# Sums in place between a quad's first products, and six second products in one run, in the experts of a fused attention, mixture and feed-forward kernel

## The chip, the cores and the metric

The kernel runs on one core of one Trainium2 chip. The metric is the device time of one execution, in microseconds. The profile comes from one execution recorded by the hardware profiler; its engines are PE (the matrix engine; PEld is its loading of weights), DVE (the vector engine), ACT (the scalar engine), POOL (GpSimd) and SP (the queue that issues most loads).

## What is computed

Three layers follow each other. An attention with random features turns `q`, `k`, `v` (4 batches, 8 heads, 576 rows, 64 columns) into 2304 rows of 512. Then a mixture of eight experts, in which every expert sees every row and a table `P` of weights (made by eight rounds of row and column scaling) mixes them, and last a feed-forward layer with `h - tanh(h)`:

```python
logits = x @ w_gate
P = np.exp(logits - logits.max())
for _ in range(8):
    P /= P.sum(1, keepdims=True) + 1e-09
    P /= P.sum(0, keepdims=True) + 1e-09
    P *= N / E
for e in range(E):                      # E = 8, w1[e] is 512 x 1024, w2[e] 1024 x 512
    h = np.maximum(x @ w1[e], 0.0)
    out += P[:, e:e + 1] * (h @ w2[e])
...
h = x @ w_in                            # 512 x 2048
return (h - np.tanh(h)) @ w_out         # 2048 x 512
```

## The kernel before, in words

**Numbers.** Every fp32 matrix is split into a high and a low half, and each product is three matmul passes (high by high, high by low, low by high).

**The experts (about 167 to 1677 us).** The 2304 rows are cut into three blocks of 768 (`NSB`), each of two halves of 384 (`TB`). For each block the loop goes over 32 quads (8 experts, 4 each): 96 quads in all. In a quad the first matmul of the layer, `x @ w1[e]`, for 256 of the hidden columns and 768 rows, is a 2 by 2 block product, computed by Strassen's scheme in Winograd's form: seven *first products* on sums of blocks in place of eight. `product(ps, i, start, stop, last)` (L961) issues one: six matmuls of 384 columns into one of the three PSUM banks `a`, `b`, `e` of the quad; with `start=False` it adds to what lies in the bank. The scheme's own sums are made in between: some by adding further products into a bank, some by the vector engine. `quad` (L983) holds the order of a quad; its results are four tiles `h[k]`, each the positive part of a result as a high half (`relu_hi`, scalar engine, L978) and a low half (`relu_lo`, vector engine, L981, reading the bank and the high half).

**Second products.** `l2` (L1079) is one second product, 128 rows of `h @ w2[e]` for a quad's 256 hidden columns: six matmuls of 512 columns (L1074) into one of three banks `l`, followed by one accumulation on the vector engine (L1109: bank times a column of `P` plus the accumulator). A quad leaves six in the list `ready`. They are issued inside the next quad: `second(n)` (L1166) takes up to n of them from the list, and calls `tick()` after each. In `quad` it is called twice, three at a time: behind the third and behind the fifth first product.

**What else is issued, and where.** `tick()` (L1136) is called 13 times in a quad, after each first and each second product. It advances three generators by a step: `weights` (fetches raw weights on the SP queue, forms the weight sums on GpSimd, L168 to L172, and splits them: high half by ACT at L83, low half by GpSimd at L86), `xops` (rows for the next block: DMA, sums at L236 and splits on DVE), and, on three ticks of eight, a background generator. That is first `gate` (the table `P`, in the first nine quads) and then `convert` (L904), which turns the float64 weights of the last layer into fp32: 64 jobs of five steps, each step two vector instructions (L930 to L945). `turn()` issues one transpose group of finished rows where one waits. Engines take their instructions in the order in which they are issued.

**A quad's order before**, with `p0` to `p6` the first products and `l` a second one: p0 (bank a), p1 (b), p2 (e), l l l, p3 (b), p4 (a), l l l, p5 (b), p6 (e). The vector engine makes `u2_ = b + s1` after p1, `v = b + s1` and `c22 = e + v` after p3 (L1002, L1003), `b = b + s1` after p5 (L1016) and `e = e + u2_` after p6 (L1021); `s1` is ACT's copy of bank `a` after p0 (L990). p5 adds into bank `b` and so waits until the sum that reads `b` after p3 is done.

**The second layer (from 1677 us).** 24 blocks: three row blocks, four groups of four hidden tiles, two halves. `shrink` (L1031) makes one hidden tile (12 matmuls of 384 columns at L1039 into one of five banks, then a chain on ACT and DVE), four of them in a block; here a second product has 12 matmuls, and each block adds three to `ready`. The loop (L1213 to L1234) issues what exceeds a number after each `shrink`: before the change `(3, 3, 3, 2)` stay for the four of a block, so the last `shrink` of a block is followed by one second product, and the first of the next block by two.

Of the kernel before, what the change touches and what calls it, by code (L numbers as in the profile page):

```python
# [13 lines left out]
ALU = mybir.AluOpType  # L14
# [5 lines left out]
def performer_moe_kernel(ctx, tc, q, k, v, omega, wg, w1, w2, win64, wout64, out):  # L20
    nc = tc.nc
    B, H, S, D = q.shape
    M = omega.shape[0]
    NT, DM = out.shape
    E, _, FE = w1.shape
# [10 lines left out]
    NSB = NT // SBT  # L36
# [4 lines left out]
    NGM = FF // (GF * P)  # L41
# [770 lines left out]
    def qbank(name):  # L812
        return ppm.tile([P, 512], F32, tag="q", name=name)
# [4 lines left out]
    def tmp(i, name):  # L818
        return tp.tile([P, TB], F32, tag=f"t{i}", name=name)
# [138 lines left out]
    def htile(name):  # L958
        return hp_.tile([P, 2, TB], F32R, tag="h", name=name)

    def product(ps, i, start, stop, last):  # L961
        need(state["x0"] + i, ux, "x")
        u, x = u1[state["n1"]], ux[state["x0"] + i]
        m = 0
        for wi, xi in ((0, 0), (0, 1), (1, 0)):
            for c in range(2):
                nc.tensor.matmul(  # L967
                    ps[:, :TB], u[:, wi, c], x[:, xi, c], start=(start and m == 0), stop=(stop and m == 5),
                    skip_group_check=True,
                )  # L970
                m += 1
        spent1.add(state["n1"])
        state["n1"] += 1
        if last:
            spentx.add(state["x0"] + i)

    def relu_hi(h, src):
        nc.scalar.activation(h[:, 0], src, AF.Relu)  # L978

    def relu_lo(h, src):  # L980
        nc.vector.scalar_tensor_tensor(h[:, 1], src, 0.0, h[:, 0].bitcast(F32), ALU.max, ALU.subtract)  # L981

    def quad(Q, last, second):  # L983

        a, b, e = qbank(f"a{Q}"), qbank(f"b{Q}"), qbank(f"e{Q}")
        A, B, EE = a[:, :TB], b[:, :TB], e[:, :TB]
        s1, u2_, v, c22 = (tmp(i, f"t{i}_{Q}") for i in range(4))
        TT = nc.vector.tensor_tensor
        product(a, 0, True, False, last)
        nc.scalar.copy(s1, A)  # L990
        tick()
        turn()
        product(b, 1, True, False, last)
        TT(u2_, B, s1, ALU.add)  # L994
        tick()
        turn()
        product(e, 2, True, False, last)
        tick()
        turn()
        second(3)  # L1000
        product(b, 3, False, False, last)
        TT(v, B, s1, ALU.add)  # L1002
        TT(c22, EE, v, ALU.add)  # L1003
        tick()
        turn()
        product(a, 4, False, True, last)
        h = {k: htile(f"h{Q}_{k[0]}{k[1]}") for k in ((1, 1), (0, 0))}
        relu_hi(h[1, 1], c22)
        relu_lo(h[1, 1], c22)
        relu_hi(h[0, 0], A)  # L1010
        relu_lo(h[0, 0], A)
        tick()
        turn()
        second(3)
        product(b, 5, False, True, last)
        TT(B, B, s1, ALU.add)  # L1016
        tick()
        turn()
        product(e, 6, False, True, last)
        turn()  # L1020
        TT(EE, EE, u2_, ALU.add)  # L1021
        for k in ((1, 0), (0, 1)):
            h[k] = htile(f"h{Q}_{k[0]}{k[1]}")
        relu_hi(h[0, 1], B)
        relu_hi(h[1, 0], EE)
        relu_lo(h[1, 0], EE)
        relu_lo(h[0, 1], B)
        tick()
        return [h[k] for k in ((0, 0), (1, 0), (0, 1), (1, 1))]

# [105 lines left out]
    def tick():  # L1136
        next(wprep, None)
        pace[0] += 1
        if pace[3] or pace[0] % 8 == 0:
            next(xprep, None)  # L1140
        if bg and not pace[2] and (pace[1] == 1 or pace[0] * 12 % 32 < 12):
            try:
                next(bg[0])
            except StopIteration:
                bg.pop(0)

    def need(n, have, what):
        k = 0
        while n not in have:
            k += 1  # L1150
            assert k < 1000, what
            next(wprep if what == "w" else xprep)
# [3 lines left out]
    def turn():  # L1156
        if turned:
            turned.pop(0)()
# [5 lines left out]
    ready, begun = [], {}  # L1164

    def second(n):  # L1166
        for _ in range(n):
            if ready:
                ready.pop(0)()
                tick()  # L1170

    n2 = 0
    for st in stages:
        kind, s = st
        if kind == 0:
            for Q in range(NQ):
                e = Q // NQE
                if s == 0 and Q == 2 * NQE + 1:
                    while bg:
                        tick()  # L1180
                if s == 0 and Q == 2 * NQE + 3:
                    phase.close()
                    pace[1] = 3
                    bg.append(convert(phase.enter_context(tc.tile_pool(name="cvp", bufs=1))))
                    next(bg[0])
                pace[2] = pace[1] > 1 and (Q == 0 or Q >= NQ - 2 or s == 0 and Q < 2 * NQE + 4 or NQ // 4 < Q < NQ // 4 + 3)
                pace[3] = Q < 2 or Q == NQ - 1
                for i in range(7):
                    need(state["n1"] + i, u1, "w")
                    if s or Q or i < 4:  # L1190
                        need(state["x0"] + i, ux, "x")
                hh = quad(s * NQ + Q, Q == NQ - 1, second)
                second(len(ready))
                for tt in range(NTS):
                    j = tt // 3
                    ready.append(
                        lambda st=st, Q=Q, n=n2, h=hh[2 * j : 2 * j + 2], tt=tt, e=e: l2(
                            st, Q == 0, Q == NQ - 1, n, h, tt, e, tt == NTS - 1
                        )
                    )  # L1200
                n2 += 2
                if Q == NQ // 4:
                    xgo[0] += 1
            state["x0"] += 7
            if s == NSB - 1:
                pace[2] = False
                while bg:
                    tick()
                phase.close()
                w2p.append(ctx.enter_context(tc.tile_pool(name="w2x", bufs=1)))  # L1210
                thp.append(ctx.enter_context(tc.tile_pool(name="thp", bufs=2)))
        else:
            for g in range(NGM):  # L1213
                for j in range(2):
                    hh = []
                    for f in range(GF):
                        for i in range(2):
                            need(state["n1"] + 2 * f + i, u1, "w")
                            need(state["x0"] + 2 * j + i, ux, "x")
                        hh.append(shrink(state["n1"] + 2 * f, j, f"{s}_{g}_{j}_{f}"))  # L1220
                        if j:
                            spent1.update(state["n1"] + 2 * f + i for i in range(2))
                        tick()
                        turn()
                        tick()
                        end = s == NSB - 1 and g == NGM - 1 and j == 1
                        second(len(ready) - (3, 3, 3, 3 if end else 2)[f])
                    for t in range(3):
                        tt = 3 * j + t
                        ready.append(  # L1230
                            lambda st=st, g=g, n=n2, h=hh, tt=tt: l2(
                                st, g == 0, g == NGM - 1, n, h, tt, None, tt == NTS - 1
                            )
                        )  # L1234
                    if g == NGM - 1:
                        spentx.update(state["x0"] + 2 * j + i for i in range(2))
                n2 += GF
                if g == 0:
                    xgo[0] += 1
                state["n1"] += 2 * GF  # L1240
            state["x0"] += 4
# [38 lines left out]
```

## Time and profile before

| | us |
|---|---|
| median of 3 runs | 2095.52 |
| lowest and highest | 2094.87, 2095.88 |
| span of the profiled execution | 2093.0 |
| PE busy in it | 2071.2 (99%) |
| DVE busy | 1766.2 (84%) |
| POOL busy | 1456.3 (70%) |
| ACT busy | 1055.9 (50%) |

The profile records the span of its execution, from the first to the last instruction, and no time around it. The granted clock of PE is at its upper level (2.4 GHz) in the whole span. In the rows below a timeline merges instructions of one line that follow each other: start, time from the first start to the last end, and their number. Matmuls overlap, so the start of the next row and not the end of a row tells how long a run held the engine.

### The profile page before, as it was taken

To read this page: it belongs to the slowest core of one execution; us is meant where nothing else is said; L and a number is where in the kernel's file an instruction comes from. 1 tells how busy PE (TensorE), PEld (TensorE's weight loads), DVE (VectorE), ACT (ScalarE), POOL (GpSimd) and SP (SyncE) were. 2 spreads that over 40 slices of the span, in tenths; PEclk is the share of its full clock that TensorE was granted. 3 is DMA by queue.
4 is the path that set the end of the run, shared out by engine and by line. 5 is a ranking of instruction groups with operands and counts; after the bars stand their busy time and mean duration, and the time that the engine had idled before them with its cause. 6 is when DMAs were issued, how large, how long until landed. Compare 5 with 4: busy or idle time off the path is not lost.

```text
span 2093.0 us, 34243 instructions
## 1 busy us (share of the span) xinstructions
PE 2071.2 (99%) x11070; PEld 1852.7 (89%) x11070; DVE 1766.2 (84%) x3330; ACT 1055.9 (50%) x2576; POOL 1456.3 (70%) x2016
## 2 busy tenths in 40 slices
PE   9999999999999999999999999999999999999999
PEld 7777989999998999889999899999999989999997
DVE  8885868988888787899888788788875699999997
ACT  7884334333334433333333433333333388888885
POOL 7876877767777767777777767677777555665652
PEclk9999999999999999999999999999999999999999
DMA  6535213223222323223223223323222232231310
GB/s 171 138 102 174 80 62 119 86 84 104 91 86 80 114 89 126 76 84 111 83 85 106 92 88 104 106 83 104 91 70 77 71 104 75 70 121 46 111 46 31
DMA packets 184372, 195.78 MB, mean 94 GB/s; under 512 B 53376, under 2 KB 142976, under 8 KB 184192
## 3 DMA queue, kind: packets, MB, share of 16 engines
q1 hardware_dynamic: 176464, 183.91, 27.8%
q10 hardware_dynamic: 7728, 9.69, 1.4%
q8 instruction: 87, 1.43, 0.3%
q14 instruction: 93, 0.76, 0.1%
HBM read 171.00 MB, written 22.54 MB: 92 GB/s over the span
## 4 chain that ended last, share of the span: by engine, by line
PE 89%; POOL 4%; DVE 4%; ACT 1%; issue 1%; DMA 0%; ACTq 0%; POOLq 0%; DVEq 0%
PE l L1074 46%; PE b L967 14%; PE e L967 9%; PE a L967 9%; PE p L1039 9%; POOL tmp L404 2%; POOL eq L564 1%; DVE acc L1109 0%; DVE jk L551 0%; PE x L1123 0%; DVE sq L409 0%; ACT ek L440 0%; POOL nb L493 0%; POOL nm L491 0%; PE lgT L842 0%
## 5 line engine op out<-in xcount | busy, mean ns | idle before, releaser
L1074 PE MATMUL l<-v,h 128*128 128x512 f32 x4320 | 1031.1, 392 | 0.9 <-DVE second L1101 0.6
L1074 PEld LDWEIGHTS l<-v,h 128*128 128x128 f32 x4320 | 805.3, 188 | 163.0 <-ACT h L978 1.8
L86 POOL TENSOR_TENSOR v<-rs,v 128x256 fp32r<-128x256 f32 x432 | 334.9, 804 | 182.0 <-ACT v L83 172.2
L1109 DVE SCALAR_TENSOR_TENSOR acc<-l,pt,acc 128x512 f32<-128x512 f32 x516 | 376.0, 744 | 78.1 <-PE l L1074 75.5
L86 POOL TENSOR_TENSOR u<-s,u 128x256 fp32r<-128x256 f32 x384 | 292.8, 782 | 106.2 <-ACT u L83 105.8
L967 PE MATMUL b<-x,u 128*128 128x384 f32 x1728 | 351.4, 338 | 0.3 <-DVE t L994 0.3
L83 ACT CAST u<-s 128x256 fp32r<-128x256 f32 x384 | 147.0, 408 | 395.3 <-PE b L967 337.9
L967 PEld LDWEIGHTS b<-x,u 128*128 128x128 f32 x1728 | 308.6, 188 | 15.4 <-DVE t L994 0.6
L86 POOL TENSOR_TENSOR u<-rq,u 128x256 fp32r<-128x256 f32 x288 | 225.9, 784 | 128.2 <-ACT u L83 96.1
L967 PE MATMUL a<-x,u 128*128 128x384 f32 x1152 | 231.9, 335 | 1.3 <-POOL u L86 1.3
L967 PE MATMUL e<-x,u 128*128 128x384 f32 x1152 | 231.3, 335 | 0.0
L83 ACT CAST v<-rs 128x512 fp32r<-128x512 f32 x240 | 147.2, 620 | 161.4 <-PE l L1074 155.7
L1039 PE MATMUL p<-x,u 128*128 128x384 f32 x1152 | 209.8, 336 | 1.1 <-DVE th L1051 1.1
L1039 PEld LDWEIGHTS p<-x,u 128*128 128x128 f32 x1152 | 202.0, 188 | 5.1 <-DVE th L1051 1.5
L967 PEld LDWEIGHTS a<-x,u 128*128 128x128 f32 x1152 | 202.6, 188 | 2.7 <-POOL u L86 1.7
L967 PEld LDWEIGHTS e<-x,u 128*128 128x128 f32 x1152 | 202.9, 188 | 0.0
L1063 POOL TENSOR_TENSOR h<-t,h 128x384 fp32r<-128x384 f32 x96 | 98.8, 1029 | 131.3 <-ACT h L1062 124.1
L978 ACT ACTIVATE h<-b 128x384 fp32r<-128x384 f32 x96 | 47.2, 492 | 170.8 <-DVE b L1016 170.0
L83 ACT CAST u<-rq 128x256 fp32r<-128x256 f32 x288 | 117.0, 406 | 0.8 <-ACT xo L1125 0.8
L86 POOL TENSOR_TENSOR u<-rqi,u 128x256 fp32r<-128x256 f32 x96 | 85.8, 917 | 34.6 <-ACT u L83 33.0
L978 ACT ACTIVATE h<-t 128x384 fp32r<-128x384 f32 x96 | 50.4, 525 | 115.2 <-DVE t L1003 115.2
L981 DVE SCALAR_TENSOR_TENSOR h<-e,h 128x384 fp32r<-128x384 f32 x96 | 53.6, 558 | 56.5 <-ACT h L978 56.5
(178 smaller groups left out, 2997.2 us busy)
## 6 DMA issues: line engine op xcount, KB each, us to landing
rq<-in_moe_w_dram SPq DMA_DIRECT2D x96, 512.0 KB, 3.8
rs<-in_moe_w_dram SPq DMA_DIRECT2D x192, 256.0 KB, 3.1
rqi<-win SPq DMA_DIRECT2D x24, 512.0 KB, 4.4
rs<-wout SPq DMA_DIRECT2D x48, 256.0 KB, 2.7
xt<-xd SPq DMA_DIRECT2D x24, 384.0 KB, 5.4
r<-in_moe_w_in_dram SPq DMA_DIRECT2D x32, 256.0 KB, 3.2
r<-in_moe_w_out_dram SPq DMA_DIRECT2D x32, 256.0 KB, 3.3
xd<-xo SPq DMA_DIRECT2D x32, 144.0 KB, 1.8
```

The costliest lines, as they stand in the source:

```text
L83: nc.scalar.copy(dst[:, 0], src)
L86: eng.tensor_tensor(dst[:, 1, i : i + w], src[:, i : i + w], dst[:, 0, i : i + w].bitcast(F32), ALU.subtract)
L404: nc.gpsimd.tensor_tensor(tmp[:, c], t[:, c], t[:, c], ALU.mult)
L564: nc.gpsimd.tensor_tensor(eq[:n], eq[:n], dn[:n, c].to_broadcast([n, 2, M]), ALU.mult)
L967: nc.tensor.matmul(ps[:, :TB], u[:, wi, c], x[:, xi, c], start=(start and m == 0), stop=(stop and m == 5), skip_group_check=True,)
L978: nc.scalar.activation(h[:, 0], src, AF.Relu)
L981: nc.vector.scalar_tensor_tensor(h[:, 1], src, 0.0, h[:, 0].bitcast(F32), ALU.max, ALU.subtract)
L1039: nc.tensor.matmul(ps, u1[f + i][:, wi, c], ux[state["x0"] + 2 * t + i][:, xi, c], start=(m == 0), stop=(m == 11))
L1063: nc.gpsimd.tensor_tensor(lo, s, hi.bitcast(F32), ALU.subtract)
L1074: nc.tensor.matmul(ps, hh[f][:, hi, t : t + P], u2[n + f][:, wi], start=(f == 0 and i == 0), stop=(f == len(hh) - 1 and i == 2),)
L1109: V.scalar_tensor_tensor(a, ps, p[:, e : e + 1], a, ALU.mult, ALU.add)
```

## The change

In `quad`: the sum `b + s1` is written back into bank `b` after p1, before p3 is added to it, and ACT copies it to `u2_`; after p2 ACT copies bank `e` to `e2`, and `e + u2_` is written back into bank `e`. After p3 one sum, `c22 = b + e2`, remains; p5 and p6 then add to banks that hold their sums already, so that their results are read at once. The two calls `second(3)` become one `second(6)`, behind p2. The order of a quad becomes p0, p1, p2, l l l l l l, p3, p4, p5, p6. In the second layer the numbers that stay become 3 for each `shrink`, so that the three second products of a block are issued in one run, behind the first `shrink` of a block.

```diff
-        s1, u2_, v, c22 = (tmp(i, f"t{i}_{Q}") for i in range(4))
+        s1, u2_, e2, c22 = (tmp(i, f"t{i}_{Q}") for i in range(4))
         TT = nc.vector.tensor_tensor
+        h = {}
+
+        def relu(k, src):
+            h[k] = htile(f"h{Q}_{k[0]}{k[1]}")
+            relu_hi(h[k], src)
+            relu_lo(h[k], src)
+
         product(a, 0, True, False, last)
         nc.scalar.copy(s1, A)
         tick()
         turn()
         product(b, 1, True, False, last)
-        TT(u2_, B, s1, ALU.add)
+        TT(B, B, s1, ALU.add)
+        nc.scalar.copy(u2_, B)
         tick()
         turn()
         product(e, 2, True, False, last)
+        nc.scalar.copy(e2, EE)
+        TT(EE, EE, u2_, ALU.add)
         tick()
         turn()
-        second(3)
+        second(6)
         product(b, 3, False, False, last)
-        TT(v, B, s1, ALU.add)
-        TT(c22, EE, v, ALU.add)
+        TT(c22, B, e2, ALU.add)
         tick()
         turn()
         product(a, 4, False, True, last)
-        h = {k: htile(f"h{Q}_{k[0]}{k[1]}") for k in ((1, 1), (0, 0))}
-        relu_hi(h[1, 1], c22)
-        relu_lo(h[1, 1], c22)
-        relu_hi(h[0, 0], A)
-        relu_lo(h[0, 0], A)
+        relu((1, 1), c22)
+        relu((0, 0), A)
         tick()
         turn()
-        second(3)
         product(b, 5, False, True, last)
-        TT(B, B, s1, ALU.add)
+        relu((0, 1), B)
         tick()
         turn()
         product(e, 6, False, True, last)
         turn()
-        TT(EE, EE, u2_, ALU.add)
-        for k in ((1, 0), (0, 1)):
-            h[k] = htile(f"h{Q}_{k[0]}{k[1]}")
-        relu_hi(h[0, 1], B)
-        relu_hi(h[1, 0], EE)
-        relu_lo(h[1, 0], EE)
-        relu_lo(h[0, 1], B)
+        relu((1, 0), EE)
         tick()
...
-                        end = s == NSB - 1 and g == NGM - 1 and j == 1
-                        second(len(ready) - (3, 3, 3, 3 if end else 2)[f])
+                        second(len(ready) - 3)
```

## Rows read from the trace of the kernel before

**Rows 1.** The page's first part: busy time, share of the span, instructions.
```profile
PE 2071.2 (99%) x11070; PEld 1852.7 (89%) x11070; DVE 1766.2 (84%) x3330; ACT 1055.9 (50%) x2576; POOL 1456.3 (70%) x2016
```

**Rows 2.** Waits of the weight loads: total us, times, longest us.
```profile
PEld l L1074 <- ACT h L978: 1.8, 6, 0.7
PEld l L1074 <- DVE h L981: 1.7, 6, 0.3
```

**Rows 3.** Timeline of PE, 800 to 850 us: start, us, instructions.
```profile
804.12 4.28 PE L1074 MATMUL l<-v,h 128*128 128x512 f32 x18
808.24 1.23 PE L967 MATMUL b<-x,u 128*128 128x384 f32 x6
809.31 1.20 PE L967 MATMUL a<-x,u 128*128 128x384 f32 x6
810.35 4.28 PE L1074 MATMUL l<-v,h 128*128 128x512 f32 x18
...
824.88 1.20 PE L967 MATMUL a<-x,u 128*128 128x384 f32 x6
```

**Rows 4.** Timeline of PE in the second layer, 1780 to 1830 us.
```profile
1789.30 2.92 PE L1074 MATMUL l<-v,h 128*128 128x512 f32 x12
1792.06 2.27 PE L1039 MATMUL p<-x,u 128*128 128x384 f32 x12
1794.17 5.64 PE L1074 MATMUL l<-v,h 128*128 128x512 f32 x24
1799.65 6.43 PE L1039 MATMUL p<-x,u 128*128 128x384 f32 x36
```

**Rows 5.** Timeline of PE, 881 to 892 us.
```profile
881.99 0.86 PE L1074 MATMUL l<-v,h 128*128 128x512 f32 x3
...
886.73 1.23 PE L967 MATMUL b<-x,u 128*128 128x384 f32 x6
```

**Rows 6.** Groups of instructions: count, busy us, mean ns, idle us before.
```profile
L1109 DVE SCALAR_TENSOR_TENSOR acc<-l,pt,acc 128x512 f32<-128x512 f32 x516 | 376.0, 744 | 78.1 <-PE l L1074 75.5
...
L1021 DVE TENSOR_TENSOR e<-e,t 128x384 f32<-128x384 f32 x96 | 53.4, 556 | 14.6 <-PE e L967 14.5
...
L945 DVE SCALAR_TENSOR_TENSOR cx<-ct,cx 128x256 f32<-128x256 f32 x64 | 50.0, 782 | 2.2
...
L990 ACT COPY t<-a 128x384 f32<-128x384 f32 x96 | 45.9, 478 | 2.1 <-DMA xd<-xo 1.8 <-PE a L967 0.2
```

**Rows 7.** Timeline of DVE, 800 to 850 us, a quad in time.
```profile
824.02 0.75 DVE L1109 SCALAR_TENSOR_TENSOR acc<-l,pt,acc 128x512 f32<-128x512 f32 x1 [0.61 <-PE l L1074]
825.08 0.56 DVE L1002 TENSOR_TENSOR t<-b,t 128x384 f32<-128x384 f32 x1 [0.31 <-PE b L967]
```

**Rows 8.** Timeline of DVE, 166 to 196 us, the first quad.
```profile
170.66 0.56 DVE L994 TENSOR_TENSOR t<-b,t 128x384 f32<-128x384 f32 x1 [0.45 <-ACT t L990]
```

**Rows 9.** Timeline of PE, 166 to 196 us, the product that waits for it.
```profile
171.27 1.31 PE L967 MATMUL b<-x,u 128*128 128x384 f32 x6 [0.32 <-DVE t L994]
```

**Rows 10.** The line of `v`: ns min/median/max, first and last start; idle us before, times.
```profile
L1002 DVE TENSOR_TENSOR t<-b,t x96: 539/550/558, 172.8 to 1670.1; 128x384 f32<-128x384 f32 x96
...
  PE b L967: 11.8, 30
```

**Rows 11.** Timeline of DVE, 800 to 850 us, conversion steps ahead of `v`.
```profile
809.11 0.28 DVE L944 TENSOR_SCALAR ct<-ce 128x256 f32<-128x256 uint32 x1
809.43 0.42 DVE L945 SCALAR_TENSOR_TENSOR cx<-ct,cx 128x256 f32<-128x256 f32 x1
809.77 0.55 DVE L1002 TENSOR_TENSOR t<-b,t 128x384 f32<-128x384 f32 x1
```

**Rows 12.** Timeline of DVE, 866 to 925 us, a backlog.
```profile
918.69 2.06 DVE L1109 SCALAR_TENSOR_TENSOR acc<-l,pt,acc 128x512 f32<-128x512 f32 x3
...
921.44 0.55 DVE L1002 TENSOR_TENSOR t<-b,t 128x384 f32<-128x384 f32 x1
```

**Rows 13.** Timeline of PE, 917 to 926 us, the same quad.
```profile
919.41 1.20 PE L967 MATMUL a<-x,u 128*128 128x384 f32 x6
```

## The prediction

> **What bounds the kernel now.** I read the page's engine shares first: the matrix engine is busy 99% of the span, the vector engine 84%, the scalar engine 50% [rows 1]. So the time is the sum of the matmuls plus the places where the matrix engine waits. The list of waits of its weight loads comes next. In the experts they waited for the halves `h` for 1.8 and 1.7 us, in six places each [rows 2]; everything else there belongs to the attention stage or to single places. The third view is the matrix engine's timeline, where the order of the work shows. A first product (6 matmuls of 384 columns) starts 1.04 us before the next thing (809.31 to 810.35), but 1.07 us when second products came just before it (808.24 to 809.31). A group of three second products, 18 matmuls, takes 4.12 us [rows 3]. The second layer shows the same matmuls in runs of 12 and 24: 2.76 and 5.48 us [rows 4]. The 12 that differ cost 2.72, 0.2267 each, so a run pays about 0.04 us once, whatever its length (18 x 0.2267 + 0.04 = 4.12 agrees). **A break costs 0.04 on entering and 0.03 on leaving, 0.067 us together** (unrounded starts give 41 and 26 ns). A quad has two such runs, and the change makes one of them.
>
> **The gains, part by part.** (1) 96 quads, of which the first has no second products: 95 breaks x 0.067 = 6.4 us. (2) The second layer has 24 blocks; in 23 of them the run of one second product behind the fourth `shrink` goes and joins the next run: 23 x 0.067 = 1.5 us. Its `h` halves are read later but the last reader stands where it stood, so nine `h` buffers still do, and three banks serve three products. Four `shrink`s in a row on the vector engine leave it behind for a time, and the 36 matmuls after them (8.2 us) cover that: cost nothing; without that cover the wait would be at the five `p` banks. (3) The waits for `h`: the group from 881.99 took 886.73 - 881.99 = 4.74 us in place of 4.12 [rows 5], because `h10` went bank, vector sum, scalar half, vector half, behind a late vector engine. The sum now stands before the run, so the last leg is scalar and vector half only, and one sum of 0.556 us [rows 6] leaves this path. The waits add up to 3.5 us of weight loads [rows 2]; a late load costs the stream about 0.06 less than its delay (below), 12 x 0.06 = 0.7, so 2.8 us at most; I take 2.5, bounds 0 and 2.8. Sum of gains: 10.4 us.
>
> **Work that only moves.** The vector engine does three sums a quad in place of five, 1.1 us less; the scalar engine gets two copies of 0.478 us [rows 6], 0.96 us in a quad of 15.6 us at half load. That costs nothing while it has room: the copies of `b` and `e` have the run of 36 (8.2 us) to finish before the next product into `b` (L1001 before); without the run they would cost about 1 us a quad. The weight preparation moves too: the 13 ticks a quad stay 13, but six of them now stand in one run, so the two casts of `v`, released by the last second product, are issued behind products 5 and 6 and the GpSimd sums after products 0 and 1. Counted tick by tick, the units of a quad are still finished more than a quad ahead, and loads on the SP queue follow the same order; nothing waits for them.
>
> **The cost that appears: `c22`.** Before, `b`'s product 5 stood behind product 4 and 18 second products; its wait was for the sum `v`. Now only product 4, 1.04 us, stands between the end of product 3 and product 5, and product 5 waits until `c22` has read the bank. Deadline: in a quad where the vector engine is on time, product 4 starts at 824.88 [rows 3] and `v`, the same operation that `c22` now is, starts 0.20 later and ends at 825.64 [rows 7]. A product that waited for the vector engine began its weight load at 171.27, 0.05 behind the end of that sum at 171.22 [rows 8, 9]. So product 5 is released at 825.69; its load is due with product 4's last matmul, 5 x 0.173 behind 824.88, 825.75. Spare 0.06. The delayed product lasts 1.31 in place of 1.20 us [rows 3, 9]: its first matmul comes 0.11 behind the load, not 0.17 as in a running stream, another 0.06: **`c22` may be 0.12 us late for nothing, all beyond that stops the matrix engine.**
>
> How late would it be? At `v` the vector engine waited for product 3 in 30 of 96 quads only [rows 10]; in the others it came from other work. Two patterns: a pair of conversion steps right behind the last accumulation, `v` at 809.77, 0.46 behind product 4's start in place of 0.20 [rows 3, 11], cost 0.26 - 0.12 = 0.14; and a backlog, `v` at 921.44, 2.03 behind 919.41 [rows 12, 13], cost 1.7. Reading all 95 quads so: 45 cost nothing, 41 together 8.6 us, nine (the backlogs) 12.7 us. **Upper bound 21.3 us** if the lateness stays as it is; lower bound 0. But the run before `c22` is now twice as long: 8.2 us with six accumulations of 0.744 [rows 6], 4.5 us, and 2.25 pairs of steps on average (three ticks of eight), each 0.7 to 1.6 us (the second step takes 0.42 in [rows 11], 0.78 on average in [rows 6]), about 2.7 us. So 1 us of an older backlog drains in the run, and 1.1 us more per quad. What remains is the pair behind the last accumulation, in 3/8 of some 65 converting quads, 24 x about 0.1, and about 1.6 us in the gate's quads and the backlogged stretch. I take 4 us, nearer to the lower bound.
>
> **Banks.** Six second products in one run share three banks; the fourth needs the first's accumulation done. On time that has 1.8 us to spare: an accumulation ends 0.95 behind its matmuls (824.77 against 823.82, 1.06 ahead of product 4 [rows 3, 7]), and two products, 2.75 us, lie between. In the backlog the first accumulation ends at 918.69 + 0.74 = 919.43 [rows 12], and the fourth product would be due at 919.41 - 1.07 = 918.34 [rows 13], 1.1 us earlier. Some eight quads are like this, but the first wait lets the vector engine catch up: 3.5 us; bounds 0 and 12 (eight times 1.5). **The first quad** has no second products to cover the copy behind the sum that ends at 171.22 [rows 8], 0.478: 0.5 us, bounds 0 (the weights it waits for next come no earlier) and 2.
>
> **Sum.** -6.4 - 1.5 - 2.5 + 4 + 3.5 + 0.5 = **-2.4 us** on the profiled span of 2093.0, so 2090.6. The median of the runs is 2095.5; the 2.5 us that lie around the span are taken as unchanged: **2093.1 us**. A change under 0.2%, 4.2 us, is about what cannot be told from none.
>
> A rule that speaks against part (1) and (2): the runs of 12 and 24 and the 1.07 against 1.04 show a price for a break [rows 3, 4]. The Trainium skill, "TensorE: Matmul & The Clock Gate", section "Back-to-back issue gap", gives a gap from one matmul to the next that depends on its own columns alone, N/2.4 + 2.5 ns, with no term for a change of shape. By it a break would be free, the 7.9 us would go, and the sum would be 2101.0. The trace speaks against it.
>
> **The rivals.** (A) As summed: 2093.1, its own range 2089 to 2098. Chance 0.40. (B) The lighter vector engine keeps up: two sums fewer of 0.55 us a quad end the backlogs, `c22` and the banks cost 0.5 us together: -10.4 + 0.5 + 0.5 = -9.4, 2086.1; with 3 us of both 2088.6. I take 2088. For: 84% load falls to about 79%. Against: two thirds of the `v`s were not on time. Chance 0.35. (C) `c22`'s lateness stays what `v`'s was: -10.4 + 21.3 + 0.5 = +11.4, 2106.9. It decides from 14.1 us of lateness, 0.15 us a quad beyond the spare 0.12. For: 50 of 95 quads were later than that. Against: the drained backlog above. Chance 0.20. (D) A break is not what costs the 0.067 (the merged run pays the same within): 2101.0; against it stands that runs of 12, 18 and 24 all pay 0.04 once. Chance 0.05.
>
> **How the numbers follow.** Faster by over 0.2% (under 2091.3): a fifth of A and six sevenths of B, 0.38. Slower (over 2099.7): a twentieth of A, 0.85 of C and 0.7 of D, 0.23. The rest 0.39. The range reaches from B's middle, 2086, to 2102, between D and C's middle; it leaves out a seventh of B and two thirds of C, 0.19.
>
> **What would show it.** Right: runs of 36 second products of 8.20 us in one, of 36 in the second layer too; no waits for `h`; a new wait of the weight loads of `b` for the vector engine at `c22`, some 4 us, and of `l` for the accumulation at L1109's line, some 3 us, between 600 and 960 us above all. Wrong: runs of 36 near 8.24 (D), waits for `c22` in most quads (C), or none (B); or a wait of the vector engine for the scalar copy of `e` that holds up the accumulations.

## The result, and the profile after

| | before | after |
|---|---|---|
| median, us | 2095.19 (4 runs) | 2113.08 (4 runs) |
| lowest and highest | 2094.43, 2095.88 | 2112.17, 2114.77 |
| span of the profiled execution | 2093.0 | 2110.4 |
| of it up to the first product of the experts | 167.5 | 169.1 |
| experts | 1509.6 | 1517.1 |
| second layer and end | 415.8 | 424.2 |

The ratio is 1.0086, interval 1.0074 to 1.0099 at 95%. Ratios, here and below, compare the means of the runs; the one run that is left out of them is an execution of e3 that took 4981 us. The changed kernel is slower by 18 us, where 2.4 us less were forecast; the stated range ended at 2102 us. The stages add up to the 17.4 us between the spans: 1.5 in the attention, which the change doesn't touch (its length varied between executions), 7.5 in the experts, 8.4 in the second layer.

First the page's first part of the kernel after, to be read beside [rows 1]:

```profile
PE 2071.7 (98%) x11070; PEld 1849.4 (88%) x11070; DVE 1704.1 (81%) x3138; ACT 1138.2 (54%) x2768; POOL 1459.0 (69%) x2016
```

The matrix engine has the same work (2071.7 against 2071.2 us) and the vector engine 62 us less (72 less in the experts, where three sums in a quad in place of five had promised 106, and 10 more in the second layer). So the 17 us are new idle time of the matrix engine. Its weight loads name it (line waited for, total us, times, longest):

```profile
PEld b L967 <- DVE t L1012: 11.8, 22, 1.8
PEld l L1073 <- ACT h L1061: 6.4, 6, 2.6
PEld l L1073 <- DVE acc L1108: 5.6, 5, 2.5
...
PEld p L1038 <- DVE th L1050: 2.7, 1, 2.7
...
PEld l L1073 <- ACT t L1047: 2.2, 1, 2.2
```

The waits of [rows 2] are gone from the list. In their place stand `c22` (L1012) and the `l` banks (L1108) in the experts, 17.4 us together, and three rows of the second layer (L1061, L1050, L1047), 11.3 us.

What was hoped for is there all the same. The timeline of PE, kernel after, from a run of second products on (start, us, instructions):

```profile
811.82 8.36 PE L1073 MATMUL l<-v,h 128*128 128x512 f32 x36
820.02 1.23 PE L967 MATMUL b<-x,u 128*128 128x384 f32 x6
821.08 1.21 PE L967 MATMUL a<-x,u 128*128 128x384 f32 x6
822.15 1.33 PE L967 MATMUL b<-x,u 128*128 128x384 f32 x6
823.32 1.20 PE L967 MATMUL e<-x,u 128*128 128x384 f32 x6
```

The 36 matmuls hold the engine for 820.02 - 811.82 = 8.20 us, the forecast length. Measured from the first product of a quad to that of the next, 62 of the 96 quads are calm in both kernels and shorter by 0.07 us, the price of the break. In this quad, though, product 5 (822.15) is a delayed one, 1.33 long. The timeline of DVE there shows why:

```profile
820.22 0.75 DVE L1108 SCALAR_TENSOR_TENSOR acc<-l,pt,acc 128x512 f32<-128x512 f32 x1 [0.43 <-PE l L1073]
820.89 0.28 DVE L930 TENSOR_SCALAR ct<-r 128x256 uint32<-128x256 uint32 x1
821.20 0.43 DVE L931 SCALAR_TENSOR_TENSOR ch<-r,ct 128x256 uint32<-128x256 uint32 x1
821.55 0.55 DVE L1012 TENSOR_TENSOR t<-b,t 128x384 f32<-128x384 f32 x1
```

A conversion pair behind the last accumulation puts `c22` 0.47 us behind product 4's start (821.55 against 821.08), and the quad loses 0.16 us. That is the small pattern of the prediction: in 13 quads a pair stands so, and they wait 0.18 to 0.32 us each, 3.0 us together. The large waits are of another kind; the first example is a quad of the gate. DVE, then PE, kernel after:

```profile
233.54 0.68 DVE L1100 TENSOR_TENSOR acc<-l,acc 128x512 f32<-128x512 f32 x1
234.14 0.29 DVE L888 TENSOR_REDUCE rs<-pt 128x18 f32<-128x144 f32 x1
234.46 0.53 DVE L889 TENSOR_SCALAR rs<-rs 128x18 f32<-128x18 f32 x1
235.03 0.27 DVE L890 RECIPROCAL rs<-rs 128x18 f32<-128x18 f32 x1
235.32 0.48 DVE L891 TENSOR_TENSOR pt<-pt,rs 128x144 f32<-128x144 f32 x1
235.84 0.41 DVE L892 TENSOR_REDUCE cs<-pt 128x8 f32<-128x144 f32 x1
236.17 0.55 DVE L1012 TENSOR_TENSOR t<-b,t 128x384 f32<-128x384 f32 x1
```

```profile
234.18 1.21 PE L967 MATMUL a<-x,u 128*128 128x384 f32 x6
236.77 1.31 PE L967 MATMUL b<-x,u 128*128 128x384 f32 x6 [1.38 <-DVE t L1012]
```

Five steps of the gate stand between the last accumulation of the run and `c22`, and the matrix engine stops for 1.4 us. Five quads with such late sums (two of the gate, one with double accumulations at 346, two behind a change of row block, where an accumulation had waited 1.4 us for a transpose, at 711 and 1215) wait 1.0 to 1.8 us each, 7.0 together. Four single quads make up the other 1.8.

In the second layer the calm blocks gain 0.07 us as well, and a few lose 0.4 to 4 us each. Timeline of PE, kernel after, around one of them:

```profile
1869.81 8.44 PE L1073 MATMUL l<-v,h 128*128 128x512 f32 x36 [1.86 <-DVE acc L1098]
1878.09 8.51 PE L1038 MATMUL p<-x,u 128*128 128x384 f32 x48
1888.86 10.04 PE L1073 MATMUL l<-v,h 128*128 128x512 f32 x36 [2.26 <-ACT h L1061]
1898.74 6.43 PE L1038 MATMUL p<-x,u 128*128 128x384 f32 x36
```

Two blocks in a row wait about 2 us ahead of their run, and the second run then takes 9.88 us in place of 8.2. The timeline names the scalar engine for the wait at 1888.86; DVE, in the same stretch, says otherwise:

```profile
1877.38 0.54 DVE L1050 TENSOR_TENSOR th<-p,th 128x384 f32<-128x384 f32 x1
1877.85 1.29 DVE L1056 SCALAR_TENSOR_TENSOR t<-t,t 128x384 f32<-128x384 f32 x1
1879.25 0.56 DVE L1057 SCALAR_TENSOR_TENSOR t<-t,t 128x384 f32<-128x384 f32 x1
...
1888.04 1.87 DVE L1098 COPY acc<-l 128x512 f32<-128x512 f32 x3
```

The first of the three copies out of the `l` banks ends at about 1888.04 + 0.68, and the run starts 0.12 behind it: the load waited for its bank. This copy stood in the vector engine's queue behind four shrinks, which began at 1872.24.

### The profile page after: what moved, and what is told of

Same layout as the page of the kernel before. It is cut to its first block, busy times and chain, and to the rows that moved or that the text cites. A ratio compares the mean times of both kernels' runs of the same rounds, so it can differ in the third digit from the quotient of the medians.

```text
span 2110.4 us, 34123 instructions
## 1 busy us (share of the span) xinstructions
PE 2071.7 (98%) x11070; PEld 1849.4 (88%) x11070; DVE 1704.1 (81%) x3138; ACT 1138.2 (54%) x2768; POOL 1459.0 (69%) x2016
## 4 chain that ended last, share of the span: by engine, by line
PE 74%; DVE 13%; issue 4%; ACT 4%; POOL 4%; DMA 1%; SPq 0%; DVEq 0%; ACTq 0%; POOLq 0%
PE l L1073 38%; PE b L967 14%; PE e L967 9%; PE a L967 9%; DVE t L1056 2%; PE p L1038 2%; DVE t L1057 2%; DVE t L1049 2%; POOL tmp L404 1%; DVE acc L1100 1%; POOL eq L564 1%; ACT t L1055 1%; DVE v L86 1%; ACT v L83 1%; DVE acc L1108 1%
## 5 line engine op out<-in xcount | busy, mean ns | idle before, releaser
L1073 PE MATMUL l<-v,h 128*128 128x512 f32 x4320 | 1009.6, 391 | 10.0 <-ACT h L1061 4.6
L1108 DVE SCALAR_TENSOR_TENSOR acc<-l,pt,acc 128x512 f32<-128x512 f32 x516 | 377.7, 745 | 98.8 <-PE l L1073 94.7
L86 POOL TENSOR_TENSOR v<-rs,v 128x256 fp32r<-128x256 f32 x432 | 341.7, 823 | 78.8 <-ACT v L83 72.2
L967 PEld LDWEIGHTS b<-x,u 128*128 128x128 f32 x1728 | 304.7, 188 | 21.1 <-DVE t L1012 11.8
L1002 ACT COPY t<-b 128x384 f32<-128x384 f32 x96 | 46.1, 480 | 129.4 <-DVE b L1001 129.3
L1007 DVE TENSOR_TENSOR e<-e,t 128x384 f32<-128x384 f32 x96 | 54.0, 563 | 65.4 <-ACT t L1006 65.3
L1056 DVE SCALAR_TENSOR_TENSOR t<-t,t 128x384 f32<-128x384 f32 x96 | 93.9, 978 | 0.0
```

What stands on the lines that cost most here:

```text
L86: eng.tensor_tensor(dst[:, 1, i : i + w], src[:, i : i + w], dst[:, 0, i : i + w].bitcast(F32), ALU.subtract)
L967: nc.tensor.matmul(ps[:, :TB], u[:, wi, c], x[:, xi, c], start=(start and m == 0), stop=(stop and m == 5), skip_group_check=True,)
L1002: nc.scalar.copy(u2_, B)
L1056: nc.vector.scalar_tensor_tensor(s, gb, B1, s, ALU.add, ALU.mult)
L1073: nc.tensor.matmul(ps, hh[f][:, hi, t : t + P], u2[n + f][:, wi], start=(f == 0 and i == 0), stop=(f == len(hh) - 1 and i == 2),)
L1108: V.scalar_tensor_tensor(a, ps, p[:, e : e + 1], a, ALU.mult, ALU.add)
```

## The experiments

Each was timed against the kernel before on the same chip; that median was between 2095.0 and 2095.3 us throughout.

**e1 and e2: the two parts alone.** e1 is the change without its second-layer line; e2 is the kernel before with that line alone:

```diff
-                        end = s == NSB - 1 and g == NGM - 1 and j == 1
-                        second(len(ready) - (3, 3, 3, 3 if end else 2)[f])
+                        second(len(ready) - 3)
```

> The changed quads with the second layer as it was before. Theory (two separate losses): the experts lose the 7.5 us that the two traces show there (1517.1 against 1509.6 us), the second layer nothing: about 2102.7 us, between 2100 and 2105. Rival (the loss in the second layer is handed on from a vector engine that leaves the experts late): about 2111 us, and the second layer still takes some 424 us.

> The quads as before, only the second layer's three second products in one run. Theory (the second layer loses by itself, four shrinks in a row against a vector engine that is busy 92% of the layer): 2095.2 + 8.4 = about 2103.6 us, the layer some 424 us and not 416, the step at the line gb + B1 near 0.98 us and not 0.87. Rival (handed on from the experts): the saved breaks show, 2093.7 us.

e1: 2101.24 us, ratio 1.0031 (1.0020 to 1.0041). e2: 2104.58, ratio 1.0044 (1.0029 to 1.0059). Together 6.1 + 9.4 = 15.5 of the 17.9 us: both parts lose, each on its own. In e1 the waits of the experts are those of the full change, to the tenth:

```profile
PEld b L967 <- DVE t L1012: 11.8, 22, 1.8
PEld l L1073 <- DVE acc L1108: 5.6, 5, 2.5
```

and its second layer takes 414.2 us. In e2 every quad is as before, and the second layer takes 425.0.

**e3: products 5 and 6 exchanged.** e1, but product 6 (into `e`) stands before product 5 (into `b`), each with its own operands, so that two products lie between product 3 and the one that waits for `c22`:

```diff
-        product(b, 5, False, True, last)
-        relu((0, 1), B)
+        product(e, 6, False, True, last)
+        relu((1, 0), EE)
         tick()
         turn()
-        product(e, 6, False, True, last)
+        product(b, 5, False, True, last)
         turn()
-        relu((1, 0), EE)
+        relu((0, 1), B)
```

> As the quads alone, with the last two first products exchanged: product 6 (bank e) before product 5 (bank b), so that c22 has two products, 2.08 us, and not one before bank b is written again. Theory (the wait for c22 is a deadline missed by a fraction of a microsecond up to 1.9 us): the 11.8 us of waits of b's weight loads for the vector engine fall under 1.5 us, the time falls by some 9 us against the quads alone, to about 2093. Rival (the vector engine is behind as a whole in those quads): the waits move to the l banks or the h halves, and the time stays above 2100 us.

2094.06 us, ratio 0.9991 (0.9982 to 1.0001), 7.2 below e1. The waits for `c22` fall from 11.8 to 2.0 us:

```profile
PEld b L967 <- DVE t L1011: 2.0, 3, 0.9
```

So the experts' loss is mostly the short way from product 3 to product 5. One more product of 1.04 us covers most of these waits (under 1.5 us had been expected to stay). What is left stands in single quads, 2.6 us of wait for a second product at most.

**e8: more breaks.** The kernel before with three runs of two second products in place of two runs of three (the third call of `second(2)` stands behind product 3):

```diff
-        second(3)
+        second(2)
         product(b, 3, False, False, last)
...
+        second(2)
         product(a, 4, False, True, last)
...
-        second(3)
+        second(2)
         product(b, 5, False, True, last)
```

> The kernel before with a quad's second products in three runs of two (behind the third, fourth and fifth first product) in place of two runs of three: one break more per quad, nothing else. Theory (a break costs 0.067 us): 95 more are 6.4 us, about 2101.6 us, a quad on time 15.64 and not 15.57 us. Rival (a break costs nothing): 2095 us.

2099.16 us, ratio 1.0020 (1.0010 to 1.0029). Every calm quad is longer by 0.07 us. The price of a break holds when a break is added as when one is removed; rival D falls. (Ninety-five times 0.067 is 6.4; the time rose by 4, since the waits of the second products went in this order too.)

**e4 and e5: the sums and the run apart.** e4 is the change with `second(3)` twice, in the old places, and the old second layer: sums in place, runs of three. e5 has the old sums and the run of six, and the old second layer:

```diff
-        second(6)
+        second(3)
         product(b, 3, False, False, last)
...
+        second(3)
         product(b, 5, False, True, last)
```

> The sums in place and the copies on the scalar engine, but the second products in two runs of three as before; second layer as before. Theory (the loss in the experts is the one run of six: it takes the cover from c22 and asks more of the three l banks): no waits of b's weight loads for c22, the waits for h gone, 2095.2 - 2.5 = about 2092.5 us. Rival (the new chain through the scalar engine, bank e copied before its sum, holds up the vector engine): still above 2099 us.

> The sums as before (u2_, v, c22 and the two late ones), but the six second products in one run; second layer as before. Theory (the run, not the sums, makes the loss, and the lighter vector engine of the new sums helps a little): b's weight loads wait for v by 13 to 20 us in total, about 2104 us, above the 2101.2 of the quads alone. Rival (the sums in place make the loss): 2089 to 2095 us.

e4: 2093.74 us, ratio 0.9991 (0.9981 to 1.0001). e5: 2111.13, ratio 1.0073 (1.0058 to 1.0089). So the run makes the loss, and the sums in place alone are worth about 1.5 us at most, but about 10 us under the run (2111.1 against e1's 2101.2), 7 us more than I had expected of e5. The waits of e5 show where:

```profile
PEld l L1073 <- DVE acc L1108: 16.2, 24, 3.2
PEld b L967 <- DVE t L1002: 11.4, 21, 1.8
```

At bank `b` e5 waits as long as e1; at the `l` banks it waits 16.2 in place of 5.6 us. The two vector sums that are saved in a quad were worth nothing where I had looked for them, at `c22`, and paid at the accumulations.

**e6 and e7: GpSimd's subtraction taken away in the second layer.** e6 is e2, e7 the kernel before, each with the low half of `h` in the second layer set to zero in place of the subtraction:

```diff
-            nc.gpsimd.tensor_tensor(lo, s, hi.bitcast(F32), ALU.subtract)
+            nc.gpsimd.memset(lo.bitcast(F32), 0.0)
```

> The second layer's change alone, and the low half of h, that GpSimd makes by a subtraction, is left out: GpSimd writes zeros there in its place, reading nothing. Theory (four shrinks in a row leave the vector engine so late that its step at gb + B1 runs beside GpSimd's subtraction and takes 0.94 us in place of 0.87, and that is what makes it too slow for the three l banks): the step falls to some 0.6 us, the waits of l's weight loads vanish and the saved breaks show, 2092 to 2095 us. Rival (it is the order alone: an accumulation stands between the vector engine and the next four shrinks): the waits stay, over 2100 us.

> The control for that: the kernel before with the same low half left out. Both theories: the matrix engine is the bound there already, 2093 to 2096 us, with the vector engine some 30 us less busy in the second layer.

e6: 2092.81 us, ratio 0.9987 (0.9976 to 0.9997). e7: 2092.50, ratio 0.9986 (0.9976 to 0.9997). Without the subtraction the new order costs nothing: of the waits of e2's second layer one of 1.4 us at a `p` bank is left, and its calm blocks are 0.07 us shorter. It gains nothing either: the layer takes 413.2 us in e6 and 413.3 in e7. In both the vector engine is busy for 333 to 334 us of it, 81%, against 390.9 in e2, so e6 takes away much more than what the new order had added. The groups of DVE in the second layer (count, busy us, mean ns), kernel before, kernel after, e6:

```profile
L1057 DVE SCALAR_TENSOR_TENSOR t<-t,t 128x384 f32<-128x384 f32 x96 | 83.6, 870 | 0.0
```

```profile
L1056 DVE SCALAR_TENSOR_TENSOR t<-t,t 128x384 f32<-128x384 f32 x96 | 93.9, 978 | 0.0
```

```profile
L1057 DVE SCALAR_TENSOR_TENSOR t<-t,t 128x384 f32<-128x384 f32 x96 | 52.5, 547 | 0.0
```

This is one and the same step, the first of a shrink that reads two SBUF tiles. It takes 0.55 us alone, 0.87 on average before, 0.98 after. The extra time is a wait for GpSimd; its timeline beside the step at 1877.85 shown above, kernel after:

```profile
1877.71 1.02 POOL L1062 TENSOR_TENSOR h<-t,h 128x384 fp32r<-128x384 f32 x1 [1.14 <-ACT h L1061]
```

The subtraction ends at 1878.73, the step at 1879.14, 0.41 later. Over all 96 steps this lag is 0.41 to 0.42 wherever at least 0.3 us of a subtraction were left when the step began, save one. That is so for 50 steps before (1.09 us on average) and for 73 after (1.10). The 23 more, at 1.10 - 0.55 us, are 12.6 us of vector engine; the group's sum rose by 10.3. The Trainium skill, "SBUF — State Buffer", section "Who interferes with whom", has the rule: VectorE with two SBUF inputs and a GpSimd operation that reads SBUF exclude each other for a whole instruction, and a GpSimd operation that only writes doesn't count. The traces agree, the 547 ns beside the zeroing included.

**e10: a fourth bank.** e2, with the third second product of a block in one of the five banks that otherwise serve the `shrink`s in this layer:

```diff
-            ps = lbank("l2")
+            ps = (qbank if kind and tt % 3 == 2 else lbank)("l2")
```

> The second layer's change alone, with the third second product of each three in one of the banks of the other pool, so that the three l banks serve two products a block and one bank in five serves the third. Theory (the loss is the wait for an l bank whose accumulation stands behind four shrinks on a late vector engine): the waits of l's weight loads fall under 1.5 us, 2093 to 2096 us, though the vector engine's steps stay as slow as in the run without it (0.9 us and more at gb + B1). Rival (the vector engine is the bound of the layer as a whole, and banks only show it): the waits move to the banks p, over 2100 us.

2103.14 us, ratio 1.0039 (1.0025 to 1.0053): 1.4 us below e2. The waits left the `l` banks and came up at the `p` banks:

```profile
PEld p L1039 <- DVE th L1051: 4.8, 6, 1.4
PEld p L1039 <- DVE acc L1099: 4.1, 1, 4.1
```

My theory, that a fourth bank would end the waits, fell. The vector engine is behind, and the bank that it frees last shows it. The test isn't a clean one, though: the layer has no bank more than before, and the `shrink`s share one of their five. So what more banks would be worth stays open.

**e12: more vector work in the old order.** The kernel before with one small copy ahead of that first two-tile step:

```diff
+        nc.vector.tensor_copy(s[:, :64], s[:, :64])
         nc.vector.scalar_tensor_tensor(s, gb, B1, s, ALU.add, ALU.mult)
```

> The kernel before, in its old order, with one small vector operation more in each shrink of the second layer: 64 columns of s copied onto themselves ahead of the step with gb, 96 times some 0.1 us. Nothing is left out. Theory (the second layer loses because the vector engine, without room there, has 8 to 10 us more to do, not because of the order itself): the time rises by 4 to 9 us, the median comes out at 2099 to 2104, and the matrix engine's weight loads wait for the vector engine in the second layer. Rival (the order makes the loss: four shrinks in a row with nothing between them): in the old order 10 us more of vector work change the time by under 2 us, 2095 to 2097, and no such waits appear.

2113.49 us, ratio 1.0087 (1.0070 to 1.0104): 18 us, all in the second layer, more than the theory allowed. The copy was no operation of 0.1 us. Groups of DVE, second layer of e12:

```profile
L1059 DVE SCALAR_TENSOR_TENSOR t<-t,t 128x384 f32<-128x384 f32 x96 | 72.8, 759 | 11.1 <-ACT t L1048 0.9 <-ACT th L1049 0.5
L1058 DVE SCALAR_TENSOR_TENSOR t<-t,t 128x384 f32<-128x384 f32 x96 | 54.7, 570 | 10.0
...
L1057 DVE COPY t<-t 128x64 f32<-128x64 f32 x96 | 44.0, 459 | 0.0
```

It takes 0.17 us at least and 0.46 on average: it now is what waits for GpSimd, and the step behind it falls to 0.57. With its neighbours, whose sum went from 229.3 to 249.0 us (copy included), and 10 us of gaps behind it, the vector engine had about 30 us more to do, less 6 on weight splits that went faster. The rival (the order alone) falls as far as this: in the old order too, more vector time in the second layer becomes waits of the matrix engine, by more than half. The forecast size was wrong.

**e9 and e11: a better version.** e9 is e3 with two runs of three where the run of six had waited (the first 13 quads, and the first and last of a row block), and the old second layer; e11 is e9 with e10's second layer:

```diff
-        second(6)
+        second(3 if split else 6)
         product(b, 3, False, False, last)
...
+        second(3)
+        product(e, 6, False, True, last)
...
-                hh = quad(s * NQ + Q, Q == NQ - 1, second)
+                hh = quad(s * NQ + Q, Q == NQ - 1, second, Q in (0, NQ - 1) or s == 0 and Q < 13)
```

> The exchanged products of before (e last but one, b last) with one run of six only where the vector engine has room: in the first 13 quads and in the first and the last quad of each row block the second products stay in two runs of three. Second layer as before. Theory (what was left of the loss with the exchange lies in the quads of the gate and of the row splits, 0 to 10, 32 and 63): those lose nothing now, some 80 quads gain 0.07 us each, about 2088 us (2086 to 2090), faster than both. Rival (the lateness only moves into the next quads): 2092 to 2095 us.

> Both together: the exchanged products with one run of six where there is room, and the second layer's three in one run with the third in a bank of the other pool. If both theories hold: 2088 - 1.5 = about 2086.5 us. If the second layer's loss stays: about 2097 us.

e9: 2090.19 us, ratio 0.9977 (0.9968 to 0.9986), 5 us below the kernel before and 23 below the changed one: the fastest of this case, just above the 2086 to 2090 that had been expected. The experts take 1504.7 us in its trace, against 1509.6. e11: 2098.13, ratio 1.0016 (1.0007 to 1.0024); the second layer's three in one run cost about 8 us here too.

## Why the prediction was wrong, point by point

**The gains of the experts were right.** 0.067 us a quad is what 62 quads show, and e8 pays it in reverse. Three of the quads that had waited for `h` are shorter by 0.24 to 0.32 us beyond it, and one that had waited 0.7 us for an accumulation by 0.82: 1.7 us against the 2.5 taken, though half of it is not the `h` that was named.

**`c22`: the right wait, but in other quads and larger.** The step that failed is the rest that was to stay, "about 1.6 us in the gate's quads and the backlogged stretch", and with it the 4 us taken. Measured were 11.8 us of waits in 22 quads; apart from the first quad they made theirs longer by 10.7 us than the saved break allows. (Where nothing else differs, a wait lengthens its quad by 0.02 us less than it lasts, and `c22` could be 0.11 us late for nothing; the prediction had 0.06 and 0.12.) The small pattern was priced well in sum, 2.6 us against 2.4, but by luck: 13 quads of 0.2 us where 24 of 0.1 had been counted.

The older backlog did drain, as foretold. The engine was on time in 66 quads against 30 [rows 10], and in the nine quads that had been late in the kernel before, `c22` is at most 0.47 us behind product 4. The quad of [rows 12, 13], 2.03 us behind there, in the kernel after:

```profile
930.77 1.20 PE L967 MATMUL a<-x,u 128*128 128x384 f32 x6
931.24 0.55 DVE L1012 TENSOR_TENSOR t<-b,t 128x384 f32<-128x384 f32 x1
```

The large waits are new lateness, in other quads. In four of the five the `v` of the kernel before was no more than 0.20 us behind product 4, in the fifth (at 346) 0.76. The quad that waits at 236.77, in the kernel before:

```profile
227.63 1.29 PE L967 MATMUL a<-x,u 128*128 128x384 f32 x6
227.70 0.56 DVE L1002 TENSOR_TENSOR t<-b,t 128x384 f32<-128x384 f32 x1 [0.37 <-PE b L967]
```

There it was 0.07 behind; `c22` is 1.99 behind (236.17 against 234.18), since the gate's five steps now stand between the run's last accumulation and it. So reading how late `v` had been could neither price `c22` nor bound it: by that reading these five quads were to cost 0.4 us, and they cost 6.9. e3 shows that the short cover was the other half of the cause, since one product more takes most of the waits away.

**The banks:** 5.6 us of waits against 3.5 taken, within the bounds; e5 shows that without the saved sums it would have been 16.2. In one of them, at 687.67, where the matmuls stood for 2.1 us, the accumulations stood behind the new wait of `e`'s sum for the scalar copy, which I had named as a way to be wrong. It is 0.93 us there as in 43 of the 96 quads, where it costs nothing; here two row splits (3.1 us) had made the sums late before. **The first quad** lost 1.4 us and the second won 1.5.

By the lengths of the quads, the terms account for the experts: -6.4 for the breaks, -1.7 for the four quads above, +10.7 for `c22` and +4.8 for the four other quads with a wait for a bank are 7.4; the stage is longer by 7.5.

**The second layer: the step that failed is "cost nothing".** I had written that four shrinks in a row "leave it behind for a time, and the 36 matmuls after them (8.2 us) cover that". That takes a vector engine with room, and I read its load from the whole span, 84% [rows 1]. In this stage it is 92%. The two rows (start:end, us, busy PE, PEld, DVE, ACT, POOL, granted clock, DMA share, GB/s) are those of the kernel before and the kernel after:

```profile
1677.20:2093.00 415.80, 409.99 (x2077) 371.93 (x2075) 382.49 (x588) 330.89 (x726) 231.86 (x236) 1.00 0.23 76
```

```profile
1686.20:2110.40 424.20, 411.75 (x2077) 372.20 (x2075) 392.31 (x586) 329.23 (x723) 229.07 (x235) 1.00 0.22 74
```

And the new order gave it 10 us more to do: nothing stands between the shrinks any more, so 73 of the 96 first steps fall onto a subtraction of GpSimd where 50 had. The backlog then lasts for blocks, and it shows at the `l` banks and the `p` banks, 11.3 us of waits. The term was -1.5 and came out at +8.4 (e2: +9.4 in the time). e6 shows that without any of these collisions, with the vector engine busy 81% of the layer, the order costs nothing; e12 shows that in the old order more vector time suffices for such waits. That it is the 23 further collisions that tip the balance is argued from the two, not shown: no run took away these alone.

**The rivals.** None covered both halves. C had the sign and 11.4 of the 18 us, but by a lateness that stays what it was, and that had gone. D is refuted by the runs of 8.20 us and by e8. The Trainium skill, "TensorE: Matmul & The Clock Gate", section "Back-to-back issue gap", lets the gap depend on a matmul's own columns alone. The runs differ: 0.067 us went with each break taken away and came with each one added (e8), and the measurement decides. **The range** had no term for the second layer at all: with the vector engine at 92% there, an upper bound above nothing was due for "cost nothing", and the range would have reached higher.

## What to carry to other kernels

Read an engine's load in the stage in which the change puts more on it in a row, not over the span: at 92% a reordering without any new work was enough to stop the matrix engine. A longer run of one kind saves its breaks exactly as measured, but all that waits behind the run loses its spacing; move the dependent product further away first (one product of 1.04 us took 7 us off the time here), then make the run longer where there is slack, and leave it split where there is none. An operation that is moved should also be looked at beside the engine that shares its memory port.

## What the hardware showed that I had not expected

- A vector step that reads two SBUF tiles and begins with 0.3 us or more of a GpSimd subtraction still to run ends 0.41 us after it, however early it began; in e12 a copy of 64 columns ended 0.05 us after it, and lasted up to 0.95 us in place of 0.17.
- After the matrix engine had stood for 2.3 us, its granted clock was 0.59 on average over the next 4.2 us, the lower of its two levels for most of it (1888.8 to 1893.0, kernel after), and the run lost 1.7 us more. How long the engine had stood did not decide it: after 2.4 us at 1732.93 in the same trace, and after 2.1 us at 687.67, the clock was 1.00. After 3.5 us in e12 it was 0.50 over 5.3 us, and 12 matmuls of 512 columns took 5.26 us (1882.21 to 1887.47) in place of 2.76. The rows of the two lower stretches:

```profile
1888.80:1893.00 4.20, 4.14 (x11) 3.31 (x12) 3.99 (x8) 2.53 (x6) 2.34 (x3) 0.59 0.88 307
```

```profile
1882.10:1887.40 5.30, 5.19 (x12) 4.14 (x13) 4.99 (x9) 3.41 (x7) 3.47 (x4) 0.50 0.11 31
```

- Waits that the list puts down to the scalar engine (L1061) were waits for a bank, as far as the distances tell: the load began 0.11 to 0.12 us behind the end of a vector copy or sum out of an `l` bank in all six, while the scalar engine's cast had ended 0.04 to 0.09 us before.
